# A fused FFT convolution, mixture of experts and bilinear layer: the inverse table is transposed on chip, and steps are placed anew

## The chip, the cores and the metric

The kernel runs on one core of a Trainium2 chip. The metric is the device time of one execution in microseconds, as the median of several runs. TensorE (PE) multiplies matrices, VectorE (DVE), ScalarE (ACT) and GpSimd (POOL) work on elements, and SyncE (SP) does nothing here but start transfers; ACT and POOL start some too. Each engine works through its own instructions in a fixed order and waits on semaphores for the others.

## The reference

```
# filter: x is (8, 3072, 256), filt_r and filt_i are (1537, 256)
X = rfft(x, axis=1);  y = irfft(X * (filt_r + 1j * filt_i), n=3072, axis=1)
x = y.reshape(24576, 256)

# experts: 8 of them, 768 slots each, filled in the order of the tokens
logits = x @ w_gate
e = argmax(logits);  g = softmax(logits)[e]
out = g * (relu(x @ w1[e]) @ w2[e])  if the token got a slot, else 0

# last layer, on all 24576 rows
result = ((out @ w_a) * (out @ w_b)) @ w_out
```

All numbers are f32. A row of zeros stays zero in the last layer.

## The kernel before

With 768 slots for each expert, the first tokens fill all of them. The kernel therefore filters and routes only the first three batches (`NB0 = 3`, 9216 tokens), works on the 6144 tokens that have slots, and writes zeros elsewhere. It counts on the way that every expert is full; if one is not, `general_path` does the rest. In these runs `fast_path` does all.

**The filter.** A transform of 3072 points is one of 128 points (step A, a product with `wa`) and one of 24 points (step B, tables `wb`). A batch has two halves of 128 channels each, and a half has eight chunks of four frequency pairs. For a chunk, `fwd` (L309) makes the spectrum with `wb`, DVE multiplies it with the filter in three instructions (L320 to L322, tiles `fr` and `fi`), POOL adds the two products into `y` (L323), and `inv` (L332) goes back with the tables `wbi`. `idft_t` (L373) turns the result and makes the logits with `iw`, and `idft_a` (L390) is the way back through step A, whose result goes to memory as `rows`. Batch 0 is transformed straight from chip memory (`dft_a_direct`, L277, and transposes with `ident`, L300); batches 1 and 2 go through memory (`dft_a`, L264, tile `da`).

**The loads.** `p1_loads` gives the transfers in the order in which SP starts them. Here they stand one behind another: half of x of batch 0, the tables of its first chunks, the other half, the other tables (four each of `wb` and `wbi`), the filter, small constants, and then batch 1 of x. Each filter tile `fr` has its real part twice, in partitions 0 to 63 and 64 to 127; the second copy is made by ACT (`twice`, L215), but for the first tile of either half, which has one row of its own and is loaded again from `fr0` (L213).

**The order of the work.** It is written out by hand. `seq` is a list of steps i, each with a forward chunk and, two steps later (`LAG`), the way back of the same chunk; three steps after batch 0 have no forward chunk (`GAP`). `put(first, last, ...)` spreads other work evenly over steps first to last: the loads of x, step A of the next batch, and for a finished batch the rest of its filter, its routing and its slots. Routing (`route`, steps s0 to s5) finds the expert and the slot of each token; a scan (s2, L426) counts tokens, s2b (L433) adds counts of other partitions. Slots are entered by eight pairs of `put` (one-hot masks and values on DVE and POOL, L468 to L471) and `add` (a product on PE, L480, and an addition on DVE, L483). When two batches are done, `early_slots` gives the first block of the first three experts, so that they can start while batch 2 is routed.

**The experts.** There are 16 blocks of 384 slots, each of eight steps s. A step makes one chunk of 128 hidden units, in three products for each f32 product (high and low parts, L666 to L668). `load_block` fetches rows with gathers on POOL (L646) and turns them on PE (L657); `load_chunk` loads weights and splits them on ACT (L633) and POOL (L634). Before the first step a list `main` has the last eight steps of `idft_t` of batch 2 with the first gather and turns; the lists `beside[s]` have what is left of batch 2: twelve row products `a`, routing `r`, slots `p` and `d`. From step 17 the weights of the last layer are converted beside the experts, and then comes the last layer.

## Time and profile before

| what | value |
|---|---|
| median of 3 runs | 1127.32 us (1125.75 to 1127.71) |
| profiled execution | 1124.34 us |
| its span, first to last instruction | 1122.5 us |
| busy: PE, PE's weight loads | 95%, 91% |
| busy: DVE, ACT, POOL | 74%, 39%, 60% |
| chain of waits that ended last | PE 80%, DMA 6%, DVE 4%, POOL 2% |

The profile is of one execution, and times in it are counted from the start of its span. It lists, among other things, windows of time with each engine's busy share and PE's granted clock (1.00 is 2.4 GHz, 0.5 is 1.2 GHz), the waits of each engine with what ended them, and the chain of work that ended last, followed back from the end. In the filter and expert stages PE has most work, in the last layer PE is busy nearly without a break.

The filter of the three batches takes up to some 225 us of the span, the experts up to some 540 us, the last layer the rest.

### The profile page before, as it was taken

To read this page: it belongs to the slowest core of one execution; us is meant where nothing else is said; L and a number is where in the kernel's file an instruction comes from. 1 tells how busy PE (TensorE), PEld (TensorE's weight loads), DVE (VectorE), ACT (ScalarE), POOL (GpSimd) and SP (SyncE) were. 2 spreads that over 40 slices of the span, in tenths; PEclk is the share of its full clock that TensorE was granted. 3 is DMA by queue.
4 is the path that set the end of the run, shared out by engine and by line. 5 is a ranking of instruction groups with operands and counts; after the bars stand their busy time and mean duration, and the time that the engine had idled before them with its cause. 6 is when DMAs were issued, how large, how long until landed. Compare 5 with 4: busy or idle time off the path is not lost.

```text
span 1122.5 us, 19362 instructions
## 1 busy us (share of the span) xinstructions
PE 1068.8 (95%) x6908; PEld 1023.9 (91%) x6908; DVE 828.7 (74%) x1589; ACT 442.6 (39%) x894; POOL 673.9 (60%) x676
## 2 busy tenths in 40 slices
PE   7899998899998999999999999999999999999993
PEld 7777797869998999999899999999999999999992
DVE  1738788675575777663888888888888888888873
ACT  2664544454665555553322232232232223232220
POOL 1412645576899787751555756657567475675742
PEclk8999999999999999999999999999999999999997
DMA  9955824354777666550404013040030000100000
GB/s 217 216 198 175 260 60 162 112 188 119 237 229 216 214 199 198 166 178 28 154 1 141 30 43 113 15 142 29 17 140 15 29 29 3 42 15 1 29 1 31
DMA packets 109097, 123.27 MB, mean 110 GB/s; under 512 B 8576, under 2 KB 92544, under 8 KB 108992
## 3 DMA queue, kind: packets, MB, share of 16 engines
q1 hardware_dynamic: 93152, 87.34, 26.4%
q10 hardware_dynamic: 11232, 22.02, 5.4%
q0 software_dynamic: 4608, 12.59, 3.6%
q8 instruction: 56, 0.92, 0.3%
q14 instruction: 49, 0.40, 0.1%
HBM read 68.44 MB, written 53.48 MB: 109 GB/s over the span
## 4 chain that ended last, share of the span: by engine, by line
PE 80%; DMA 6%; DVE 4%; issue 4%; POOL 2%; SPq 1%; ACT 1%; ACTq 0%; DVEq 0%; POOLq 0%
PE ps L666 13%; PE ps L667 13%; PE ps L668 13%; PE po L831 6%; PE po L830 6%; PE po L829 5%; PE yp L667 3%; PE yp L668 3%; PE yp L666 3%; PE ps L373 3%; PE ps L332 3%; PE ps L309 3%; PE ps L390 2%; PE ps L264 2%; DMA fr<-fr 1%
## 5 line engine op out<-in xcount | busy, mean ns | idle before, releaser
L758 POOL TENSOR_TENSOR gl<-w_b,gh 128x384 fp32r<-128x384 f32 x190 | 194.3, 1033 | 196.0 <-ACT gh L757 195.8
L757 ACT CAST gh<-w_b 128x384 fp32r<-128x384 f32 x192 | 98.7, 514 | 262.3 <-DVE w_b L776 196.8
L831 PE MATMUL po<-w_outh,gl 128*128 128x256 f32 x576 | 160.6, 279 | 0.2 <-POOL gl L758 0.2
L830 PE MATMUL po<-w_outl,gh 128*128 128x256 f32 x576 | 160.8, 279 | 0.0
L829 PE MATMUL po<-w_outh,gh 128*128 128x256 f32 x552 | 154.0, 279 | 0.0
L323 POOL TENSOR_TENSOR y<-t,t 112x512 f32<-112x512 f32 x48 | 65.6, 1368 | 128.0 <-DVE t L322 100.7
L634 POOL TENSOR_TENSOR wl<-raw,wh 128x512 fp32r<-128x512 f32 x88 | 112.3, 1292 | 39.6 <-ACT wh L633 16.5
L666 PE MATMUL ps<-th,w_bh 128*128 128x384 f32 x336 | 114.7, 341 | 4.4 <-DVE w_a L769 4.4
L666 PE MATMUL ps<-th,w_ah 128*128 128x384 f32 x336 | 113.5, 338 | 1.3 <-DVE w_b L769 0.8
L667 PE MATMUL ps<-tl,w_ah 128*128 128x384 f32 x336 | 113.6, 338 | 1.0 <-DVE tl L723 0.5
L668 PE MATMUL ps<-th,w_al 128*128 128x384 f32 x336 | 113.3, 337 | 0.0
L667 PE MATMUL ps<-tl,w_bh 128*128 128x384 f32 x336 | 113.2, 337 | 0.0
L668 PE MATMUL ps<-th,w_bl 128*128 128x384 f32 x336 | 113.1, 337 | 0.0
L683 DVE SCALAR_TENSOR_TENSOR hl<-ps,hh 128x384 fp32r<-128x384 f32 x128 | 70.5, 553 | 55.6 <-ACT hh L682 44.6
L831 PEld LDWEIGHTS po<-w_outh,gl 128*128 128x128 f32 x576 | 108.1, 188 | 1.5 <-POOL gl L758 0.4
L830 PEld LDWEIGHTS po<-w_outl,gh 128*128 128x128 f32 x576 | 108.0, 187 | 0.0
L829 PEld LDWEIGHTS po<-w_outh,gh 128*128 128x128 f32 x552 | 103.6, 188 | 0.0
L682 ACT ACTIVATE hh<-ps 128x384 fp32r<-128x384 f32 x128 | 62.7, 490 | 94.3 <-PE ps L668 84.3
L790 ACT COPY p<-ps 128x384 f32<-128x384 f32 x96 | 46.0, 479 | 127.3 <-PE ps L668 69.9
L776 POOL TENSOR_TENSOR w_b<-w_b,w_a 128x384 f32<-128x384 f32 x94 | 93.8, 1019 | 0.0
L666 PE MATMUL ps<-xh,wh 128*128 128x384 f32 x256 | 91.1, 356 | 0.0
L667 PE MATMUL yp<-hl,wh 128*128 128x384 f32 x256 | 86.0, 336 | 3.9 <-DVE hl L683 3.9
(157 smaller groups left out, 2801.3 us busy)
## 6 DMA issues: line engine op xcount, KB each, us to landing
out<-wide SPq DMA_DIRECT2D x48, 512.0 KB
raw<-w SPq DMA_DIRECT2D x176, 128.0 KB
rows<-yt ACTq DMA_DIRECT2D x18, 512.0 KB
da<-sa ACTq DMA_DIRECT2D x12, 512.0 KB
sb<-da SPq DMA_DIRECT2D x32, 192.0 KB
yd<-yb ACTq DMA_DIRECT2D x16, 384.0 KB
y<-yd SPq DMA_DIRECT2D x8, 768.0 KB
sd<-x SPq DMA_DIRECT2D x12, 256.0 KB
```

Source lines behind the costliest of these rows:

```text
L323: eng.tensor_tensor(y, t1, t2, ALU.add)
L634: (eng or nc.gpsimd).tensor_tensor(l, T["raw"], h.bitcast(F32), ALU.subtract)
L666: mm(out, wh, xh, start=first, stop=False)
L667: mm(out, wh, xl, start=False, stop=False)
L668: mm(out, wl, xh, start=False, stop=last)
L683: nc.vector.scalar_tensor_tensor(hl, hp[:, :BLK], 0.0, hh.bitcast(F32), ALU.max, ALU.subtract)
L757: nc.scalar.copy(gh, g)
L758: (v if hurry and not ij[1] else nc.gpsimd).tensor_tensor(gl, g, gh.bitcast(F32), ALU.subtract)
L776: (v if hurry or ij in ON_V else nc.gpsimd).tensor_tensor(c, c, T["a"][ij], ALU.mult)
L829: mm(out, gh[:, sl], oh[:, o:o + D], start=False, stop=False)
L830: mm(out, gh[:, sl], ol[:, o:o + D], start=False, stop=False)
L831: mm(out, gl[:, sl], oh[:, o:o + D], start=False, stop=u == NU - 1 and i == 1 and j == 0)
```

## The change

It has three parts.

*The loads.* The four `wbi` tables are not loaded. The forward table is scaled (by the square root of 2 at one frequency group) so that the way back uses its transpose, and `back_table` makes each `wbi` tile from the `wb` tile with eight transposes on PE and two copies out of PSUM on DVE. It is put into steps 1 to 8, one table in every second step. The second load of the two first filter tiles is replaced by a copy on ACT and the load of a single row, on ACT's queue. Loads of x and of tables stand in another order, and the second half's step A of batch 0 moves from steps 0 to 5 to steps 3 to 6.

*Batch 1.* Its row products and routing go from four steps to six, its slot values and additions from four to six, and `early_slots` moves by three steps to the last one.

*The experts' first steps.* The first block's turns go behind all of `idft_t`, the logits and two row products. In the lists `beside`, the row products go to one per step, the routing moves by three steps, the slot values by four, the additions by five, the gather of the third block from step 2 to step 7, and `all_slots` from step 11 to step 14.

```
-                wb[:, g, 0, 0, 0, q] = c
-                wb[:, g, 0, 1, 0, q] = -sn
-                wbi[0, 0, q, 0, :, g] = 2 * c
-                wbi[1, 0, q, 0, :, g] = -2 * sn
+                wb[:, g, 0, 0, 0, q] = 2 ** 0.5 * c
+                wb[:, g, 0, 1, 0, q] = -2 ** 0.5 * sn
...
         def real(h, i):
             t = self.fr[4 * h + i]
             q.dma_start(t[0:64], io["fr"][:, h, 8 * i:8 * i + 8, :])
+            self.twice[h, i] = lambda: twice(t, h, i)
+
+        def twice(t, h, i):
+            self.nc.scalar.copy(t[64:P], t[0:64])
             if i == 0:
-                q.dma_start(t[64:P], io["fr0"][:, h])
-            else:
-                self.twice[h, i] = lambda: self.nc.scalar.copy(t[64:P], t[0:64])
+                self.nc.scalar.dma_start(t[64:65, 0, :], io["fr0"][:, h])
...
-                steps += [lambda i=i: table("wb", i)] * (h == 0)
+                steps += [lambda i=i: table(i)] * (h == 0)
                 steps += [lambda h=h, i=i: real(h, i)] * (h + i > 0)
                 steps += [lambda h=h, i=i: imag(h, i)]
-                steps += [lambda i=i: table("wbi", i)] * (h == 0)
...
+    def back_table(self, i):
+
+        nc = self.nc
+        for k in range(0, 8, 4):
+            pt = self.ps()
+            for j in range(4):
+                nc.tensor.transpose(pt[0:M2, 96 * j:96 * j + 96], self.wb[i][:, k + j, :], self.ident[0:96, 0:96])
+            nc.vector.tensor_copy(self.wbi[i][:, k:k + 4, :].rearrange("p j r -> p (j r)"), pt[0:M2, 0:384])
...
-            if c % 2 and (h, c // 2 + 1) in self.twice:
-                self.twice.pop((h, c // 2 + 1))()
+            if c % 2 and divmod(4 * h + c // 2 + 1, 4) in self.twice:
+                self.twice.pop(divmod(4 * h + c // 2 + 1, 4))()
...
-        for step in loads[:6]:
+        for step in loads[:3] + consts[:2] + [lambda: K.twice.pop((0, 0))()] + loads[3:6]:
             step()
         K.ident_ids()
-        for step in consts[:5] + loads[6:] + consts[5:]:
+        for step in consts[2:7] + loads[6:9] + consts[7:10] + loads[9:] + consts[10:]:
             step()
...
-        put(0, 5, K.dft_a_direct(xs, sa, 1))
+        put(3, 6, K.dft_a_direct(xs, sa, 1))
+        put(1, 8, [lambda i=i: K.back_table(i) for i in range(4)])
...
-                put(5, 7, xl)
+                put(8, 10, xl)
...
-                put(i + 2, i + 5, rows_and_routes(a, r))
-                put(i + 6, i + 9, p, into=early)
-                put(i + 8, i + 11, d)
-                put(i + 12, i + 12, [K.early_slots, lambda: K.counts(r1, 0, NE, min(cap, BLK))])
+                put(i + 2, i + 7, rows_and_routes(a, r))
+                put(i + 8, i + 13, p, into=early)
+                put(i + 10, i + 15, d)
+                put(i + 15, i + 15, [K.early_slots, lambda: K.counts(r1, 0, NE, min(cap, BLK))])
...
         for k in range(8):
-            main += t1[k:k + 1] + {0: cs[0:1], 1: cs[1:2], 3: first[1:2], 4: first[2:3], 5: cs[2:3],
-                                   6: xs[1][0:1], 7: r[0:1] + cs[3:4]}.get(k, [])
+            main += t1[k:k + 1] + {0: cs[0:1], 2: cs[1:2], 5: cs[2:3], 6: xs[1][0:1]}.get(k, [])
+        main += r[0:1] + a[0:2] + first[1:2] + cs[3:4] + first[2:3]
...
-        beside[2] += xs[2][0:1]
-        for k, step in enumerate(a):
-            beside[k * 2 // 3].append(step)
+        beside[7] += xs[2][0:1]
+        for k, step in enumerate(a[2:]):
+            beside[k].append(step)
         for k, step in enumerate(r[1:]):
-            beside[k].append(step)
+            beside[3 + k].append(step)
         for k in range(0, NPUT, 2):
-            beside[7 + k // 2] += d[k:k + 2]
-            beside[6 + k // 2] += p[k:k + 2]
-        beside[11] += [lambda: K.all_slots(r1), lambda: K.counts(r1, 1, E, cap)]
+            beside[10 + k // 2] += p[k:k + 2]
+        for k in range(NPUT):
+            beside[12 + k // 3] += d[k:k + 1]
+        beside[14] += [lambda: K.all_slots(r1), lambda: K.counts(r1, 1, E, cap)]
```

The first place is the head of SP's queue. `sd` is x of batch 0, `fr`, `fi` and `wb` are the filter and the tables. Before:

```order
L249 DMA sd_89<-x 128x4x128 x6
L165 DMA ident_72<-eye 128x128
L166 DMA ids_69<-ids 128x24
L211 DMA fr0_127<-fr 64x1024
L213 DMA fr0_127<-fr0 64x1024
L207 DMA wb0_119<-wb 96x896
L219 DMA fi0_135<-fi 48x1024
L207 DMA wbi0_123<-wbi 112x768
L249 DMA sd_89<-x 128x4x128 x6
L207 DMA wb1_120<-wb 96x896
L211 DMA fr1_128<-fr 64x1024
```

After:

```order
L247 DMA sd_89<-x 128x4x128 x3
L199 DMA fr0_127<-fr 64x1024
L247 DMA sd_89<-x 128x4x128 x3
L153 DMA ident_72<-eye 128x128
L154 DMA ids_69<-ids 128x24
L195 DMA wb0_119<-wb 96x896
L209 DMA fi0_135<-fi 48x1024
L195 DMA wb1_120<-wb 96x896
L199 DMA fr1_128<-fr 64x1024
L209 DMA fi1_136<-fi 48x1024
L247 DMA sd_89<-x 128x4x128 x3
L195 DMA wb2_121<-wb 96x896
```

The two second copies `fr0` and the tables `wbi` are gone from the queue, the first filter tile stands among x, and the second table stands ahead of the second half of x.

The second place is PE's first chunks of batch 0. `sa0` is the result of step A, `sb` a chunk of it, `y` the filtered spectrum. Before:

```order
L309 MATMUL ps2_242<-sb_228,wb0_119 112x128 x4
L277 MATMUL ps_253<-wa_87,sd_89 128x128 x4
L300 MATMUL ps2_260<-ident_72,sa0_109 96x128 x4
L309 MATMUL ps_267<-sb_235,wb0_119 112x128 x4
L277 MATMUL ps2_278<-wa_87,sd_89 128x128 x4
L300 MATMUL ps_285<-ident_72,sa0_109 96x128 x4
L309 MATMUL ps2_291<-sb_259,wb1_120 112x128 x4
L332 MATMUL ps_303<-wbi0_123,y_248 128x96 x4
L277 MATMUL ps2_309<-wa_87,sd_89 128x128 x4
L300 MATMUL ps_316<-ident_72,sa0_109 96x128 x4
L309 MATMUL ps2_323<-sb_284,wb1_120 112x128 x4
```

After:

```order
L307 MATMUL ps2_238<-sb_224,wb0_119 112x128 x4
L298 MATMUL ps_250<-ident_72,sa0_109 96x128 x4
L307 MATMUL ps2_257<-sb_231,wb0_119 112x128 x4
L232 MATMUL ps_268<-ident_72,wb0_119 112x96 x4
L232 MATMUL ps2_274<-ident_72,wb0_119 112x96 x4
L298 MATMUL ps_281<-ident_72,sa0_109 96x128 x4
L307 MATMUL ps2_287<-sb_249,wb1_120 112x128 x4
L330 MATMUL ps_299<-wbi0_123,y_244 128x96 x4
L298 MATMUL ps2_306<-ident_72,sa0_109 96x128 x4
L307 MATMUL ps_313<-sb_280,wb1_120 112x128 x4
L275 MATMUL ps2_324<-wa_87,sd_89 128x128 x4
L330 MATMUL ps_330<-wbi0_123,y_263 128x96 x4
```

The products of step A (`wa`) have left these steps, and the first table's transposes (L232, from `wb0`) stand between the second forward chunk and the third; the first product of the way back, `wbi0`, stands behind the third forward chunk as before, and its table is now made and not loaded.

The third place is PE's handover from the filter to the experts. `sc` is the filtered result of batch 2, `rowt` the gathered rows, `xh` and `xl` their parts. Before:

```order
L373 MATMUL ps_2081<-iw_111,sc_1787 128x136 x3
L373 MATMUL ps2_2087<-iw_111,sc_1787 128x136 x3
L657 MATMUL ps_2093<-ident_72,rowt_2028 128x128 x3
L373 MATMUL ps2_2099<-iw_111,sc_1787 128x136 x3
L657 MATMUL ps_2105<-ident_72,rowt_2028 128x128 x3
L373 MATMUL ps2_2111<-iw_111,sc_1787 128x136 x3
L373 MATMUL ps_2121<-iw_111,sc_1787 128x136 x3
L373 MATMUL ps2_2139<-iw_111,sc_1787 128x136 x3
L412 MATMUL ps_2145<-z_1755,wai_110 128x192 x2
L390 MATMUL ps_2165<-sd_1756,wai_110 128x512
L390 MATMUL ps_2168<-sd_1756,wai_110 128x512
L666 MATMUL ps_2179<-xh_2038,wh_2067 128x384
```

After:

```order
L371 MATMUL ps_2139<-iw_111,sc_1804 128x136 x3
L371 MATMUL ps2_2145<-iw_111,sc_1804 128x136 x3
L371 MATMUL ps_2155<-iw_111,sc_1804 128x136 x3
L371 MATMUL ps2_2173<-iw_111,sc_1804 128x136 x3
L410 MATMUL ps_2179<-z_1777,wai_110 128x192 x2
L388 MATMUL ps2_2186<-sd_1778,wai_110 128x512
L388 MATMUL ps_2189<-sd_1778,wai_110 128x512
L655 MATMUL ps2_2193<-ident_72,rowt_2074 128x128 x3
L655 MATMUL ps_2203<-ident_72,rowt_2074 128x128 x3
L388 MATMUL ps_2218<-sd_1778,wai_110 128x512
L664 MATMUL ps_2221<-xh_2084,wh_2113 128x384
L665 MATMUL ps_2221<-xl_2085,wh_2113 128x384
```

The two turns with `ident` stood among the `iw` products; now they stand behind the last of these, behind the logits and two row products with `wai`.

## Rows read from the trace of the kernel before

**Rows 1.** Windows: busy time of each engine, granted clock, DMA share, GB/s.

```profile
core 0: us, PE busy (x) PEld busy (x) DVE busy (x) ACT busy (x) POOL busy (x), PEclk, DMA share, GB/s
24.00:52.00 28.00, 24.62 (x220) 24.23 (x220) 20.62 (x30) 19.34 (x29) 12.66 (x10) 1.00 0.96 195
162.00:212.00 50.00, 45.67 (x317) 39.03 (x315) 45.41 (x90) 20.48 (x38) 24.52 (x28) 0.97 0.31 100
188.00:196.00 8.00, 6.75 (x46) 6.75 (x46) 6.38 (x11) 1.51 (x4) 7.00 (x10) 0.79 0.07 19
214.00:285.00 71.00, 65.08 (x369) 56.51 (x368) 40.37 (x90) 36.31 (x78) 51.78 (x52) 1.00 0.53 165
```

**Rows 2.** DMA issues by line: tiles, queue, number of transfers, size of each.

```profile
fr<-fr SPq DMA_DIRECT2D x10, 256.0 KB
wbi<-wbi SPq DMA_DIRECT2D x4, 336.0 KB
```

**Rows 3.** Chain of waits at batch 1's first products: start us, us, what.

```profile
50.79 4.22 DMA sd<-x
55.15 3.75 PE ps L264 x4
...
60.30 1.75 PE ps L264 x4
```

**Rows 4.** Timeline of PE, one chunk: start us, us, instructions, idle before.

```profile
42.55 0.60 PE L300 MATMUL ps<-ident,sa 128*96 128x128 f32 x4
42.99 1.04 PE L309 MATMUL ps<-sb,wb 96*112 96x128 f32 x8
43.86 1.03 PE L332 MATMUL ps<-wbi,y 112*128 112x96 f32 x8
```

**Rows 5.** Timeline of DVE: first filter product, two consecutive chunks, a PSUM copy.

```profile
17.29 0.69 DVE L320 SCALAR_TENSOR_TENSOR t<-ps,fi 48x512 f32<-48x512 f32 x1 [16.13 <-PE ps L309]
...
41.95 0.69 DVE L320 SCALAR_TENSOR_TENSOR t<-ps,fi 48x512 f32<-48x512 f32 x1
...
44.12 0.69 DVE L320 SCALAR_TENSOR_TENSOR t<-ps,fi 48x512 f32<-48x512 f32 x1
...
81.12 0.55 DVE L378 COPY sd<-ps 128x384 f32<-128x384 f32 x1
```

**Rows 6.** Timeline of PE and ACT: first way-back product, first second copy.

```profile
26.11 1.03 PE L332 MATMUL ps<-wbi,y 112*128 112x96 f32 x8
...
27.08 1.04 ACT L215 COPY fr<-fr 64x1024 f32<-64x1024 f32 x1 [5.68 <-DMA fr<-fr]
```

**Rows 7.** Waits of PE, 0 to 270 us: us in total, times, longest us.

```profile
PE ps L264 <- DMA sd<-x: 4.6, 1, 4.6
...
PE ps L332 <- POOL y L323: 3.4, 1, 3.4
PE ps L433 <- DVE tot L428: 2.7, 1, 2.7
PE ps L657 <- DMA rowt<-rows,early: 1.9, 2, 1.3
```

**Rows 8.** The three scans (ns min/median/max), and POOL's timeline at the third.

```profile
L426 DVE TENSOR_TENSOR_SCAN cum<-scm,oh x3: 548/559/4741, 98.9 to 229.8; 128x192 f32<-128x192 f32 x3
...
229.13 4.95 POOL L634 TENSOR_TENSOR wl<-raw,wh 128x512 fp32r<-128x512 f32 x4
```

**Rows 9.** Handover: last sum y, third gather in the chain, first expert product.

```profile
212.69 1.28 POOL L323 TENSOR_TENSOR y<-t,t 112x512 f32<-112x512 f32 x1 [1.16 <-DVE t L322]
...
216.94 4.40 DMA rowt<-rows,early
...
226.91 0.74 PE L666 MATMUL ps<-xh,wh 128*128 128x384 f32 x1
```

**Rows 10.** Timeline of POOL and ACT: gather of the fourth block, cast of its rows.

```profile
279.22 1.03 POOL L646 DMA_INDIRECT rowt<-rows,gidx  x1 [0.15 <-issue]
...
288.48 0.48 ACT L658 CAST xh<-ps 128x384 fp32r<-128x384 f32 x1 [0.37 <-PE ps L657]
```

26 lines of the change are left out of this document (8 added, 18 removed).

## The prediction

> **What bounds the kernel now.** The page's busy shares came first: PE is busy 95% of the span, and the chain of waits that ended last is 80% PE. So an edit pays only where PE stands still or runs at its lower clock, and the question is where it does. The windows show three places before the experts are in full swing, and the change touches all three. The list of PE's waits names what ended them [rows 7].
>
> First place, the end of the loads: PE waits 4.6 us for batch 1 of x [rows 7], whose first tile lands at 50.79 + 4.22 = 55.0 us; the four products after that take 3.75 us, and the same four a little later 1.75 us [rows 3]: 2.0 us more, at the lower clock. All queues were full until then, with a DMA share of 0.96 at 195 GB/s [rows 1], so fewer bytes mean an earlier batch 1.
>
> Second, 162 to 212 us: PE is idle for 4.3 of 50 us, and from 188 to 196 its mean clock is 0.79, worth another 8 x 0.21 = 1.7 us. But VectorE (DVE) is busy 45.41 us there [rows 1]. PE's largest wait is 3.4 us, for POOL's sum, which stands behind DVE's products [rows 7]: DVE is the bound here, with 4.6 us left to gain at most.
>
> Third, the handover to the experts: 1.9 us for gathered rows and 2.7 us for the total of a scan [rows 7]. What PE waits for later than that the change leaves alone.
>
> **Part 1, the loads.** Four wbi tables of 336 KB and two copies of 256 KB go [rows 2]: 1.90 MB, at 195 GB/s [rows 1] 9.7 us of queue. Batch 1's first tile would land near 45.5 us. What is late next is PE itself, since it gets work. I follow PE from the first product of the way back, which starts at 26.11 us [rows 6], to batch 1's first product, for which PE is ready at 55.15 - 4.6 = 50.6 us [rows 3, 7]: 24.5 us.
>
> That first product now waits for its table, and the table for DVE. DVE's first filter product starts at 17.29 us [rows 5]; the first wb table comes earlier, but a ScalarE copy of 1.04 us [rows 6] now stands ahead of the first chunk, and I let these cancel (bounds: 1.5 us either way). Then DVE must do two chunks of 2.17 us (the period of L320) and two PSUM copies of 0.55 us [rows 5]: 17.3 + 4.3 + 1.1, with 0.5 for hops, 23.2 us. That is 2.9 us sooner than now, because chunk 2 no longer waits for its late forward table.
>
> Behind it PE gets more: six of the eight groups of four transposes, priced as the existing group that starts at 42.55, with the next instruction at 42.99 [rows 4]: 6 x 0.44 = 2.6 us. And two groups of step A, which used to lie ahead of that point, at the 0.87 us of a group of four [rows 4]: 1.7 us. So PE is ready at 23.2 + 24.5 + 4.4 = 52.1 us, by then the tile has long landed, and PE has not idled, so that the slow products go too. In place of 55.15 + 2.0 = 57.2 us: **5.1 us gained**. Bounds: 9.7 if the transposes and copies find idle time everywhere, 0 if DVE's eight extra copies (8 x 0.55 = 4.4) go in full onto its chain. The extra copy for the second half and the one-row load on ScalarE's queue have cover: PE is ahead of ScalarE by a chunk there. A load on SP that reuses that row's semaphore can wait for ScalarE; 6 us of margin between 45.5 and 52.1 hide it.
>
> **Part 2, batch 1's rows and slots.** No work goes or comes; twelve row products and the routing are spread from four chunks over six, the slot products from four over six. DVE's load per chunk falls where it piled up, and PE is no longer blocked while DVE catches up. Since DVE binds, the gain is DVE's own idle time, 0 to 4.6 us [rows 1]; I take two thirds, **3 us**, because a piece of the idle time is chunks in which the row products kept PE from feeding DVE, and that is what the spreading ends.
>
> The slot table now closes with the last chunk, so the first gather starts later against the last forward chunk. In the kernel before, the last sum y ends at 212.69 + 1.28 = 213.97 us and the third gather lands at 216.94 + 4.40 = 221.34 [rows 9]: 7.4 us. The expert's first product starts at 226.91, 12.9 us after y, and 1.9 of it is the wait for the gather. The change puts all of the idft steps, the logits and two row products ahead of the turns. Without the wait and the 2 us or so of turns and splits, 9 us of PE work cover 7.4 us of gather. So **1.9 us gained**; the cover is 1.6 us, and beyond it the gather is late and the gain goes (bounds 0 and 1.9).
>
> **Part 3, the experts' first steps.** The scan takes 4.74 us instead of 0.56 because, as the rows stand, it runs through four POOL splits in a row, 4.95 us [rows 8]; PE waits 2.7 us for what follows it [rows 7]. POOL had those four splits queued up behind gathers. After the change the scan comes at step 4, one step ahead of its use as now, and the gather for the third block is at step 7, so POOL should have two splits at a time and not four: 2 x 1.24 = 2.5 us of blocking in place of 4.95. I take **1.7 us** of the 2.7 as gained (bounds 0 and 2.7).
>
> The Trainium skill (SBUF — State Buffer, Who interferes with whom) says that DVE and GpSimd share one port pair under an exclusive lock held for one whole instruction. By that the scan would lose at most one split, about 1.2 us, and no wait would be left: 2.7 instead of 1.7. The row speaks against it, as the scan sat out four.
>
> Against that, slot products move from steps 6 to 9 to steps 10 to 13, nearer to the step-14 gather. That gather starts at 279.22 and its rows are cast at 288.48 [rows 10], 9.3 us for a gather that needs about 7.4 (above): nearly 2 us of lead. POOL is busy 51.78 of 71 us in this part [rows 1], and PE's time there shrinks by some 4. I put **0.8 us lost** (bounds 0 and 3).
>
> **The sum.** 5.1 + 3 + 1.9 + 1.7 - 0.8 = 10.9 us. The profiled execution took 1124.34 us, span 1122.5 and 1.84 around it; it would become 1113.4. The median of the runs, 1127.32, lies 2.98 above that execution, so the median would be 1116.4.
>
> **Rivals.** *DVE stays the bound.* It has 45.4 us of work for 50 us, and its work is the same; if spreading only moves the waits, part 2's 3 us are lost, and with them part 3's gain, as POOL has the same work in less time: 5.1 + 1.9 - 0.8 = 6.2, so 1121.1 us. For it speaks that DVE's work per chunk with slot products is as long as PE's.
>
> *The loads were hidden, or PE's new work takes the gain.* If the first table waits for DVE and each later one too, part 1 gives nothing: 10.9 - 5.1 = 5.8, so 1121.5 us. Against it: PE stood idle for 4.6 us there and the table copies are one chunk ahead of their use from chunk 4 on.
>
> *More than forecast.* PE idles nowhere up to the loads' end (8 us gained), DVE closes its gaps (4.6), the scan does not wait (2.7): 8 + 4.6 + 1.9 + 2.7 = 17.2, so 1110.1 us.
>
> *Slower: the clock stays low.* Before batch 1, PE now waits for a chain through DVE and does transposes among its products. If the granted clock stays at 1.2 GHz instead of 2.4 from the first chunk to the end of that stage, the 34 us of PE work from 17 to 52 us take twice as long. The gain of 5.1 turns into a loss of about 29, and with the other 5.8 gained the time is some 1150 us. A clock that is low for only part of it costs half of that stretch; it decides above 22 us at the low clock (half of which is the whole 10.9). Against it: with a transpose group in each step, 24 to 52 us runs at clock 1.00 and PE is busy 24.62 of 28 us [rows 1].
>
> The Trainium skill (TensorE: Matmul & The Clock Gate, Part 4: PE-mode transpose) says that transposes do not count as activity of PE for the clock as products do, which would favour this rival. The same row is evidence that a mix with products keeps the clock.
>
> **How the numbers follow.** Forecast (1112.5 to 1119.5): 0.58. DVE stays the bound: 0.16. Load gain lost: 0.10. More: 0.08. Slower by the clock: 0.05. The rest, 0.03, is a gain eaten by things not seen here. The range goes from 1109, the rival with more, to 1122.5, past the two with about half the gain; the slow clock is left out. A measurement of this kernel tells about 0.2%, 2.3 us, from no change. Faster: 0.58 + 0.16 + 0.10 + 0.08, less a little for rivals added to each other, 0.90; slower 0.06; same 0.04.
>
> **What would show it.** Right: no wait of PE on x before its first product on batch 1, which starts near 52 us at full clock; the first way-back product near 23 us; a window of 50 us before the last chunk with DVE idle for under 2.5 us; no wait on the early gather; the wait on the scan's total under 1.2 us. Wrong: that wait on x still there; a granted clock near 0.5 after 24 us; a PE wait of over 2 us on the gather of the fourth block.

## The result, and the profile after

| | before | after |
|---|---|---|
| median (executions) | 1126.53 us (4; 1124.44 to 1127.71) | 1110.46 us (4; 1109.49 to 1111.44) |
| profiled execution, its span | 1124.34 us, 1122.5 us | 1111.44 us, 1109.7 us |
| ratio after : before, 95% interval | | 0.9859, 0.9840 to 0.9879 |

The change gains 15.9 us (13.6 to 18.0). Forecast were 10.9 us and a median of 1116.4; 1110.46 lies in the range of 1109 to 1122.5, near its lower end, but below the 1112.5 to 1119.5 that had most of the chance. The sign and the places were right, the sizes too small.

PE's waits up to 270 us in the changed kernel (in total, times, longest); left out are 1.2 us at the start, which the kernel before has too, and two waits of 0.2 us. Lines are numbered two lower than before.

```profile
PE ps L330 <- POOL y L321: 2.2, 3, 1.1
PE ps L330 <- DVE wbi L233: 1.7, 1, 1.7
PE ps L298 <- ACT sa L276: 1.4, 2, 0.7
PE ps L275 <- DMA sd<-x: 1.3, 2, 1.0
...
PE ps L478 <- POOL val L468: 1.1, 1, 1.1
...
```

Against [rows 7], batch 1 of x, the scan's total and the early gather are gone from the list, and so are 2.9 us for forward tables (PE's L309 on `wb`, which [rows 7] leaves out); POOL's sum `y` costs 2.2 us in three waits instead of 3.4 in one. What came in their place is 1.7 us for the first table made on chip, and 1.1 us for slot values from POOL.

The first way-back product and batch 1's first product on PE, and DVE's first filter product and its first copies of a table:

```profile
21.37 1.86 PE L330 MATMUL ps<-wbi,y 112*128 112x96 f32 x8 [1.69 <-DVE wbi L233]
...
51.33 1.88 PE L262 MATMUL ps<-sd,wa 128*128 128x512 f32 x4
```

```profile
16.50 0.69 DVE L318 SCALAR_TENSOR_TENSOR t<-ps,fi 48x512 f32<-48x512 f32 x1 [15.35 <-PE ps L307]
...
20.67 1.01 DVE L233 COPY wbi<-ps 112x384 f32<-112x384 f32 x2
```

Windows of the changed kernel. The last one is the 50 us before its last forward chunk.

```profile
core 0: us, PE busy (x) PEld busy (x) DVE busy (x) ACT busy (x) POOL busy (x), PEclk, DMA share, GB/s
20.00:24.00 4.00, 2.63 (x13) 2.63 (x14) 3.72 (x7) 1.21 (x2) 1.37 (x3) 0.69 1.12 237
24.00:28.00 4.00, 4.00 (x34) 4.00 (x33) 2.07 (x3) 1.20 (x3) 1.35 (x2) 0.88 1.17 219
24.00:52.00 28.00, 27.32 (x243) 26.66 (x242) 19.93 (x31) 18.90 (x29) 10.39 (x9) 0.98 0.93 207
148.53:198.53 50.00, 48.21 (x359) 42.03 (x358) 45.82 (x91) 22.96 (x45) 26.23 (x28) 1.00 0.35 109
```

And the three scans (ns min/median/max), with POOL's splits beside the third:

```profile
L424 DVE TENSOR_TENSOR_SCAN cum<-scm,oh x3: 548/548/627, 92.7 to 226.0; 128x192 f32<-128x192 f32 x3
```

```profile
224.95 2.78 POOL L632 TENSOR_TENSOR wl<-raw,wh 128x512 fp32r<-128x512 f32 x2 [1.74 <-ACT wh L631]
```

The way back starts at 21.37 us instead of 26.11 [rows 6], batch 1 at 51.33 and at once at full speed, four products in 1.88 us instead of 3.75 [rows 3]. The third scan takes 0.63 us instead of 4.74, beside two splits instead of four [rows 8].

**Where the time came from.** Four marks can be followed through all kernels: DVE's first filter product of chunk 36 (of 48, counted from 0) and of the last chunk, 47; the 15th residual `hl` of the experts; and the last of the 128 `hl`. Before, then after, the range at the end of the last row being the first and the last start:

```profile
163.27 0.69 DVE L320 SCALAR_TENSOR_TENSOR t<-ps,fi 48x512 f32<-48x512 f32 x1 [0.30 <-PE ps L309]
...
210.43 0.69 DVE L320 SCALAR_TENSOR_TENSOR t<-ps,fi 48x512 f32<-48x512 f32 x1
...
277.24 0.56 DVE L683 SCALAR_TENSOR_TENSOR hl<-ps,hh 128x384 fp32r<-128x384 f32 x1 [1.52 <-ACT hh L682]
...
L683 DVE SCALAR_TENSOR_TENSOR hl<-ps,hh x128: 535/554/558, 229.3 to 529.2; 128x384 fp32r<-128x384 f32 x128
```

```profile
157.05 0.69 DVE L318 SCALAR_TENSOR_TENSOR t<-ps,fi 48x512 f32<-48x512 f32 x1 [0.30 <-PE ps L307]
...
198.53 0.69 DVE L318 SCALAR_TENSOR_TENSOR t<-ps,fi 48x512 f32<-48x512 f32 x1
...
261.82 0.56 DVE L681 SCALAR_TENSOR_TENSOR hl<-ps,hh 128x384 fp32r<-128x384 f32 x1 [0.15 <-ACT hh L680]
...
L681 DVE SCALAR_TENSOR_TENSOR hl<-ps,hh x128: 541/557/560, 217.4 to 516.2; 128x384 fp32r<-128x384 f32 x128
```

The lead is 6.2 us at the first mark and has been so, to 0.05 us, since chunk 12, the first one after step A of batch 1 has begun (the expectations below call it batch 1's second chunk; it is one of batch 0's second half). Up to there it goes up and down: 6.4 us at chunk 2, as the way back starts earlier, and -0.9 at chunks 8 to 11, when PE has done the work that the change adds. It comes back between chunks 11 and 12, where the kernel before waits 4.6 us for x and loses 2.0 at the lower clock. It grows by 5.7 to the last chunk, by 3.5 to the 15th residual, and shrinks by 2.4 to the end of the experts: 13.0 us, as the profiled executions differ (12.9). The same marks in all kernels that were run, from one profile of each, in us against that one profile of the kernel before (the last column to 0.1 us):

| kernel | ratio to before (95%) | lead at chunk 36 | gained to chunk 47 | gained to 15th residual | lost to last residual |
|---|---|---|---|---|---|
| the change | 0.9859 (0.9840 to 0.9879) | 6.2 | 5.7 | 3.5 | 2.4 |
| loads_only | 0.9957 (0.9935 to 0.9978) | 8.8 | -1.0 | -4.7 | 0.7 |
| spread_only | 0.9974 (0.9955 to 0.9993) | 1.1 | 5.7 | -2.8 | 1.9 |
| steps_only | 0.9945 (0.9927 to 0.9963) | -1.8 | -1.2 | 4.1 | 1.7 |
| no_loads | 0.9892 (0.9862 to 0.9923) | 0.9 | 5.7 | 3.5 | 2.8 |
| one_table | 0.9853 (0.9829 to 0.9876) | 4.2 | 5.7 | 3.5 | 3.7 |
| bytes_back | 0.9868 (0.9839 to 0.9897) | 7.7 | 5.7 | 3.6 | 0.2 |
| tables_loaded | 0.9901 (0.9871 to 0.9930) | 0.2 | 5.7 | 3.5 | 2.6 |
| gather_at_2 | 0.9871 (0.9844 to 0.9898) | 7.0 | 5.7 | -1.4 | 1.7 |
| slots_early | 0.9904 (0.9875 to 0.9934) | 6.3 | 5.7 | -3.1 | 2.7 |
| slots_four | 0.9881 (0.9859 to 0.9903) | 6.8 | 2.6 | 4.1 | 1.5 |
| x_first | 0.9832 (0.9805 to 0.9858) | 3.9 | 5.7 | 3.5 | 1.3 |
| act_x | 0.9830 (0.9802 to 0.9858) | 8.0 | 5.7 | 3.6 | 2.3 |

With the spreading, the gain to chunk 47 repeats to 0.1 us in ten kernels, and with the new steps too that to the 15th residual in seven; without them they scatter. So does the lead at chunk 36. Four kernels have the loads of before: 0, 1.1, -1.8 and 0.9, mean 0.1. Five have the changed ones as they are: 6.2, 8.8, 7.0, 6.3 and 6.8, mean 7.0. In the last column every kernel loses against that profile of before, the kernels with the old loads too, and nearly all of it between the 51st and the 61st residual. Both kernels wait 1.8 us for `hl` there; in the kernel before the granted clock stays at 1.00, in the changed kernel it falls:

```profile
348.00:352.00 4.00, 4.00 (x15) 3.90 (x15) 2.42 (x6) 1.32 (x3) 4.00 (x3) 0.50 0.42 128
```

The profiled execution of before, at 1124.34 us, is quicker than its four others, and the changed kernel's is the slowest of its four. So 7.0 + 5.7 + 3.5 = 16.2 us is a better account of the medians' 15.9 than the pair of profiles.

### The profile page after: what moved, and what is told of

Read it like the earlier page. It is cut to its first block, busy times and chain, and to the rows that moved or that the text cites. A ratio compares the mean times of both kernels' runs of the same rounds, so it can differ in the third digit from the quotient of the medians.

```text
span 1109.7 us, 19438 instructions
## 1 busy us (share of the span) xinstructions
PE 1067.3 (96%) x6940; PEld 1024.6 (92%) x6940; DVE 831.1 (75%) x1597; ACT 444.9 (40%) x896; POOL 675.6 (61%) x676
```

## The experiments

**One part at a time.** The three parts of the change were put on the kernel before, each alone. loads_only has Part 1. Of the diffs the core is shown, and `...` marks what is left out:

```
-                steps += [lambda i=i: table("wbi", i)] * (h == 0)
...
+        put(1, 8, [lambda i=i: K.back_table(i) for i in range(4)])
```

> The kernel before with Part 1 of the change alone: the table of the way back made on chip, one row instead of the 256 KB copies, the new order of the loads, step A of the first batch later. Measured from chunk to chunk, the filter products of VectorE in the changed kernel run 6.2 us ahead of the kernel before from batch 1's second chunk up to chunk 36. Theory (the three parts add up): with this part alone the lead is the same 6.2 us at those chunks and is kept to the end, so the time falls by 6.2 us. Rival (VectorE as the bound of the stage before the last chunk swallows a lead): VectorE has 45 us of work for 50 us there, so part of the lead is lost between chunk 37 and the last, and 2 to 4 us are left at the end. Second rival (the lead is given back at the handover, where gathers and splits were the bound): PE's waits on gathered rows and on the scan grow by the lead, 0 to 2 us left.

spread_only has the spreading of batch 1:

```
-                put(i + 2, i + 5, rows_and_routes(a, r))
-                put(i + 6, i + 9, p, into=early)
...
+                put(i + 2, i + 7, rows_and_routes(a, r))
+                put(i + 8, i + 13, p, into=early)
...
```

> The kernel before with the spreading of batch 1's row products, routing and slot products alone. In the changed kernel this stretch, from chunk 37 to the last, gains 5.7 us over the kernel before. Theory (it needs the new order of the experts' first steps): the slot table closes three chunks later, with the last chunk, and the first gather follows it; in the kernel before's order the turns and the first splits come before the row products, so PE has little left to do while the gather runs. The 5.7 us are gained up to the last chunk, and PE then waits for the gathered rows some 5 to 7 us in place of 1.9: the time falls by 0 to 3 us. Rival (the parts add up): the wait stays near 1.9 us and the time falls by 5 to 6 us. Rival (VectorE stays the bound, as named in the prediction): no lead at the last chunk, and the time gets longer by the later gather.

steps_only has the experts' first steps:

```
+        main += r[0:1] + a[0:2] + first[1:2] + cs[3:4] + first[2:3]
...
-        beside[2] += xs[2][0:1]
...
+        beside[7] += xs[2][0:1]
...
```

> The kernel before with the new order of the experts' first steps alone, row products ahead of the turns, the third block's gather and the scan later, slot products later. Theory (it mends waits only): PE's wait of 1.9 us on the gathered rows and of 2.7 us on the scan's total go, and what is late next takes a little of it: the time falls by 2 to 4 us. Rival (it brings nothing by itself, since in the changed kernel the experts' part gained 0.8 us and the handover 0.3): the time falls by 0 to 1.2 us, and the waits are only replaced by other idle time of PE between the last chunk and the fourth block.

Measured: 4.8 us (2.5 to 7.3), 2.9 us (0.8 to 5.1) and 6.2 us (4.2 to 8.2) faster. The sum, 13.9, can't be told from the whole change's 15.9.

The loads alone lead by 8.8 us at chunk 36 and have 2.4 left at the end of the experts. The interval of the medians leaves room for the theory (6.2 us) and for the first rival. The second rival is right that this execution loses at the handover, but not how: PE doesn't wait longer there than before. From the last chunk to the 15th residual, before, after, and with the loads alone:

```profile
210.43:277.24 66.81, 60.75 (x352) 51.91 (x352) 39.93 (x89) 34.62 (x75) 47.72 (x48) 1.00 0.54 170
198.53:261.82 63.29, 61.14 (x363) 52.81 (x363) 41.30 (x96) 34.27 (x75) 49.13 (x50) 1.00 0.57 177
202.63:274.15 71.52, 65.40 (x356) 56.52 (x356) 41.09 (x89) 34.76 (x75) 47.41 (x48) 0.93 0.51 159
```

PE is idle for 6.1 us before and for 6.1 with the loads alone. The 4.7 us that are lost are PE's own work, 65.40 us in place of 60.75, at a clock of 0.93 in place of 1.00. In the changed kernel the clock stays at 1.00 and PE is idle for 2.2 us. The longer of the two waits with the loads alone, on DVE, POOL and PE:

```profile
221.40 6.07 DVE L419 TENSOR_TENSOR oh<-eio,am 128x192 f32<-128x192 f32 x1
```

```profile
222.01 4.97 POOL L632 TENSOR_TENSOR wl<-raw,wh 128x512 fp32r<-128x512 f32 x4
```

```profile
227.91 2.07 PE L388 MATMUL ps<-sd,wai 128*128 128x512 f32 x2 [2.59 <-DVE hl L681]
```

POOL's four splits take 4.97 us, and DVE's mask `oh` lasts 6.07 us across them (0.63 in the profile of before). Behind it stands `hl`, for which PE waits 2.59 us, and after that the granted clock was 0.50 from 228 to 232 us. In the kernel before the same row of splits fell on the scan, the next step of the routing; PE waited 2.7 us for its total, and the clock stayed at 1.00.

The spreading alone has its 5.7 us at the last chunk and gives half back, as its theory said, but the wait for the gather is 3.1 us, not 5 to 7 (the line below). In all PE is idle for less time there than before, 4.8 us; behind the wait the clock was 0.50 from 216 to 220 us, and 0.95 up to the 15th residual.

```profile
PE ps L657 <- DMA rowt<-rows,early: 3.1, 3, 1.2
```

The new steps alone end both waits, of 1.9 and 2.7 us, and gain more than was expected, 6.2 us; their profiled execution, 1125.05 us, is the slowest of the twelve and shows less. The rival, 0 to 1.2 us, is out.

**Parts 2 and 3 together.** no_loads is the changed kernel with the loads of the kernel before; of its diff:

```
-        put(3, 6, K.dft_a_direct(xs, sa, 1))
-        put(1, 8, [lambda i=i: K.back_table(i) for i in range(4)])
+        put(0, 5, K.dft_a_direct(xs, sa, 1))
```

> The changed kernel without Part 1 (loads and tables as before), that is, the spreading of batch 1 and the new order of the experts' first steps together. Alone these two gave 2.9 and 6.2 us, and Part 1 alone 4.8; the whole change about 16. Theory (in the loads' stage and at the handover the time hangs on the clock that PE is granted after it stood idle, and the new order leaves no idle stretch at the handover to give the lead back): Part 1 is worth 6 to 8 us in the company of the others, so this kernel is 8 to 10 us faster than the kernel before. Rival (the parts add up): Part 1 is worth 4.8 us here too, and this kernel is 11 us faster. Rival (Part 1 and the spreading do the same work twice, since both feed VectorE earlier): this kernel is 13 us or more faster.

Measured: 12.2 us (8.7 to 15.6), which leaves all three cases open. The marks say more: 5.7 and 3.5 us, as in the changed kernel, so neither stretch hangs on the loads. The spreading costs 2.8 us at the handover by itself and the new steps give 4.1 by themselves, but with them the spreading's later table costs only 0.6.

**What of the loads it is.** Three edits of the changed kernel. one_table makes one of the tables and uses it for all four:

```
-        put(1, 8, [lambda i=i: K.back_table(i) for i in range(4)])
+        put(1, 8, [lambda: K.back_table(0)])
```

> The changed kernel with one of the four tables of the way back made on chip and used in place of all four; six of the eight groups of transposes and six of the copies out of PSUM are left out. This prices the work that the change adds. Theory (PE binds up to batch 1's first product): six groups at 0.33 us of PE, 2.0 us, fall out of the time, and the first way-back product still comes at 21.4 us. Rival (the transposes and copies lie in idle time): no change within 0.5 us. Rival (VectorE binds there): six copies at 0.55 us, 3.3 us, fall out.

bytes_back adds transfers of the size of the dropped tables:

```
+            if h == 0:
+                extra = self.drm.tile([96, 8, M2], F32, name=f"extra{i}")
+                q.dma_start(extra, io["wb"][:, 8 * i:8 * i + 8, :])
```

> The changed kernel with 1.34 MB of extra transfers, four of 344 KB from the table of the way there into a spare place in device memory, put on SyncE's queue where the four dropped tables stood. Nothing waits for them; the tables are still made on chip. Theory (it is the bytes): at some 200 GB/s the loads end 6 to 7 us later, PE waits again for batch 1 of x by 1 to 5 us, and the time rises by 4 to 7 us, with the slow products that follow the wait. Rival (it is the order: the first way-back product no longer stands behind the second forward table, and x comes with a margin of more than 6 us): the time rises by at most 1.5 us, and there is no wait on batch 1 of x.

tables_loaded loads the tables of the way back again:

```
+            if h == 0:
+                q.dma_start(self.wbi[i], io["wbi"][:, 8 * i:8 * i + 8, :])
...
-        put(1, 8, [lambda i=i: K.back_table(i) for i in range(4)])
```

> The changed kernel with the four tables of the way back loaded, 336 KB each, as in the kernel before, and not made on chip; the one row in place of the 256 KB copies, the order of the loads, step A and all else stay as changed. In four profiles with Part 1 as changed, the filter products from batch 1's second chunk to chunk 36 run 6.2 to 8.8 us ahead of the kernel before, 7.1 on average; extra transfers within device memory took none of that. Theory (the tables made on chip are what the loads' gain comes from): with them loaded the lead there falls to 2 us or less, PE waits on batch 1 of x again for 3 us or more, and the time rises by 5 us or more. Rival (the row, the order of the loads and step A's place are the gain; the tables on chip only move the work): the lead stays at 6 us or more and the time within 1.5 us. A lead between, 3 to 5 us, divides it.

One table instead of four gains 16.6 us (14.0 to 19.3), which can't be told from 15.9. What the added work costs is read from PE's busy time between the first way-back product and batch 1's first, for which PE was ready at 50.57 us before; then come loads_only, which does all eight groups, and one_table, in whose execution everything is later, as batch 0's x came late (a wait of 2.4 us):

```profile
26.11:50.57 24.46, 23.68 (x214) 23.26 (x212) 18.59 (x27) 18.30 (x28) 10.18 (x8) 1.00 0.98 203
20.46:48.77 28.31, 27.62 (x253) 27.26 (x253) 21.71 (x34) 18.96 (x28) 10.99 (x9) 1.00 0.94 208
24.00:53.22 29.22, 27.21 (x228) 26.79 (x228) 18.90 (x28) 18.65 (x28) 10.95 (x9) 0.94 0.83 179
```

At the same clock, six groups of transposes and two of step A take 3.9 us more (28.31 - 24.46), and PE has hardly more idle time to hide them in, 0.8 us before and 0.7 after. Six groups at 0.33 us are 2.0 of it. In one_table PE's work, without some 1.7 us for four microseconds at 0.59, is 25.5 us, 2.1 less than in loads_only: the theory that PE binds has the size of the work. But that execution gives 1.3 us of it back: PE is idle for 2.0 us, all for ScalarE's copies of step A, and ScalarE had waited for a late filter tile, whose second copy stands ahead of them in its queue:

```profile
38.47 1.04 ACT L203 COPY fr<-fr 64x1024 f32<-64x1024 f32 x1 [3.51 <-DMA fr<-fr]
```

In the eight other profiles with the tables made on chip that wait is 0.68 us.

Extra transfers within device memory cost little: the lead is 7.7 us, and 14.9 us (11.6 to 18.2) are gained. Up to chunk 11 this execution runs as loads_only's to 0.01 us. Then PE waits 0.87 us before batch 1's first product:

```profile
49.80 1.96 PE L265 MATMUL ps<-sd,wa 128*128 128x512 f32 x4 [0.87 <-DVE t L321]
```

The profile names DVE's product at 49.04 us, but loads_only, whose DVE has the same product at 49.04, starts on batch 1 at 48.77, before it. So the wait is for x, issued at 45.66 us in place of 43.41, and the lead is 1.1 us smaller. The rival holds in size, not in that there is no wait.

The same tables loaded into chip memory cost the whole lead (0.2 us left, in one execution) and 4.7 us of the medians, with intervals that just overlap (7.9 to 14.6 us gained). So the row in place of the 256 KB copies and the new order give nothing without the tables made on chip that this profile shows. The theory of tables_loaded holds for the lead, misses the time by a little (5 us or more), and names the wrong place. PE does not wait for batch 1 of x; it waits for the second half of batch 0, for what ScalarE makes of it, and for forward tables (1.9 us), and loses clock behind that:

```profile
PE ps L312 <- ACT sa L290: 3.7, 2, 3.0
PE ps L289 <- DMA sd<-x: 3.3, 3, 2.5
...
```

```profile
16.00:32.00 16.00, 12.07 (x90) 11.50 (x90) 8.32 (x13) 4.08 (x6) 5.06 (x4) 0.89 1.11 223
```

ScalarE's part is again a second copy that waits for its filter tile, 7.85 us here and 4.95 at the next one, with step A's copies behind it:

```profile
31.28 1.04 ACT L215 COPY fr<-fr 64x1024 f32<-64x1024 f32 x1 [7.85 <-DMA fr<-fr]
```

The 16 us from 16 to 32 with the extra transfers in device memory:

```profile
16.00:32.00 16.00, 14.32 (x134) 14.14 (x133) 13.12 (x21) 8.60 (x13) 6.35 (x5) 1.00 1.09 272
```

At the same DMA share the loads into chip memory move 223 GB/s, and with the others beside them 272. So the loads' gain comes from tables that are not loaded, but, as far as one profile of each tells, it is not one of bytes alone. Why transfers within device memory found room there, the runs don't show.

**Who is late next: x, or PE.** SP in the changed kernel at x of batch 1; the nine small constants ahead of it start at 39.17 us:

```profile
45.81 3.65 SPq L247 DMA_DIRECT2D sd<-x  x6
```

x_first puts x ahead of them (its diff moves `load_x` besides), and act_x, whose further edit follows, has the first table's copies on ScalarE as well:

```
-        for step in consts[2:7] + loads[6:9] + consts[7:10] + loads[9:] + consts[10:]:
+        for step in consts[2:7] + loads[6:9] + consts[7:10] + loads[9:] + consts[10:-9] + xl + consts[-9:]:
```

> The changed kernel with batch 1 of x on SyncE's queue ahead of the nine small constants instead of behind them. In the changed kernel the first of x is issued at 45.81 us, after nine small loads from 39.17 us on, and PE takes up batch 1 at 51.33 us; in two of four profiles of the same code PE waited 0.5 to 0.6 us for x. Theory (PE itself is late next, as the prediction had it): x is issued near 39 us, lands by 45, no wait on x remains, and the time falls by 0.6 us at most; the lead over the kernel before at chunk 12 to 36 stays within 6.2 to 8.8 us. Rival (the margin was used up and x still sets the end of this stage): the lead grows to over 9.5 us and the time falls by 2 us or more.

```
-            nc.vector.tensor_copy(self.wbi[i][:, k:k + 4, :].rearrange("p j r -> p (j r)"), pt[0:M2, 0:384])
+            copy = nc.scalar.copy if i == 0 else nc.vector.tensor_copy
+            copy(self.wbi[i][:, k:k + 4, :].rearrange("p j r -> p (j r)"), pt[0:M2, 0:384])
```

> The changed kernel with x ahead of the constants, and with the first table of the way back copied out of PSUM by ScalarE instead of VectorE. In all profiles with the tables made on chip PE waits 1.7 us for the first table at 19.7 to 21.4 us, since VectorE's copies stand behind the second chunk's products; in one of them the granted clock then fell to 0.69 and 0.88 for the next 8 us. Theory (the VectorE copies of the first table set the start of the way back): the wait falls under 0.5 us, the first way-back product comes 1.2 us or more earlier, the clock stays at 1.00 from 16 to 52 us, and the lead at chunk 12 to 36 is 8.5 to 10 us; the time falls by 1 to 3 us against the changed kernel. Rival (PE's work up to batch 1 is bound by ScalarE's copies of step A's second half): PE's waits on those copies, 1.4 us now, grow by what the table gives, and the time stays within 1 us.

With x issued first, at 41.52 us, no wait on it is left; the lead at chunk 36 is 3.9 us, outside both forecasts, since batch 0's x came late in that execution (waits of 2.2 us) and the clock was 0.58 from 24 to 28 us. With the copies on ScalarE too, PE's wait for the table and the window after it are

```profile
20.30 1.10 PE L331 MATMUL ps<-wbi,y 112*128 112x96 f32 x8 [0.69 <-ACT wbi L234]
```

```profile
20.00:24.00 4.00, 3.71 (x34) 3.73 (x34) 3.85 (x6) 2.28 (x5) 2.35 (x2) 1.00 1.09 225
```

0.69 us instead of 1.69, the way back starts 1.1 us earlier, the clock stays at 1.00 up to 52 us, and the lead is 8.0 us: each a little short of what was expected (under 0.5, 1.2 or more, 8.5 or more), and no more than loads_only has without it. PE's waits on ScalarE's copies of step A stay at 1.4 us, so the rival is out. 19.0 and 19.2 us faster than before are the best medians of all, but their intervals (16 to 22 us) overlap the changed kernel's, so that they are better is not shown. What they show is that x doesn't set this stage any more, by more than the 0.5 to 0.9 us that three other executions waited for it.

**The scan and POOL's splits.** gather_at_2 undoes one line of the change:

```
-        beside[7] += xs[2][0:1]
+        beside[2] += xs[2][0:1]
```

> The changed kernel with the third block's gather back at the experts' step 2 instead of 7; all else as changed. In the changed kernel the scan takes 0.63 us and PE doesn't wait for its total; POOL has one or two splits in a row there. Theory (POOL's splits pile up behind the gathers, and a VectorE operation between SBUF tiles sits out the whole row of them): POOL runs three or four splits in a row around the scan's chain, one VectorE operation there takes 4 to 6 us instead of about 1, PE waits 2 to 3 us more, and the time rises by 2 to 3 us. Rival (one split at most is sat out, wherever the gather stands): the scan's chain gets longer by under 1.3 us and the time by under 1 us.

The scan on DVE, POOL's splits beside it, PE's wait, and PE's clock behind that:

```profile
225.22 5.70 DVE L424 TENSOR_TENSOR_SCAN cum<-scm,oh 128x192 f32<-128x192 f32 x1
```

```profile
224.29 6.20 POOL L632 TENSOR_TENSOR wl<-raw,wh 128x512 fp32r<-128x512 f32 x5
```

```profile
231.27 0.36 PE L431 MATMUL ps<-tot,tri 128*128 128x8 f32 x2 [2.94 <-DVE tot L426]
```

```profile
232.00:236.00 4.00, 4.00 (x14) 3.76 (x15) 1.67 (x6) 1.00 (x2) 0.70 (x1) 0.61 0.16 52
```

Five splits in a row take 6.20 us, and the scan that starts 0.9 us into them ends 0.4 us after them: 5.70 us. PE waits 2.94 us and then runs four microseconds at 0.61. Up to the 15th residual this loses 3.5 + 1.4 = 4.9 us against the changed kernel; the medians say 1.3 us, with intervals that overlap, so the 2 to 3 us of the theory are not shown in the time. In the row, the scan and the wait the theory holds, the rival with one split does not.

**The slots.** slots_early puts the last batch's routing and slots back to the steps of before:

```
-            beside[3 + k].append(step)
+            beside[k].append(step)
...
-            beside[10 + k // 2] += p[k:k + 2]
...
+            beside[6 + k // 2] += p[k:k + 2]
...
```

> The changed kernel with the last batch's routing and slot products back at the experts' steps of the kernel before (routing from step 0 instead of 3, slot products from 6 instead of 10, the slot table at 11 instead of 14); the gather at step 7 and the row products ahead of the turns stay. Theory of the prediction (slot products near the gather of the fourth block delay it): 0.8 us are gained back, up to 3, and PE's wait on that block's gather, 2.2 us in the changed kernel, shrinks below 1.5. Rival (the scan's chain meets POOL's run of three splits at step 1): PE waits 1 to 3 us for the scan's total, and the time rises by 1 to 3 us. Rival (neither matters, as PE is 15.4 us ahead of the kernel before from the first steps to the fourth block, and gives back 2.4 us only behind it, to gathers and splits on POOL): within 0.7 us.

It loses 3.5 + 3.1 = 6.6 us up to the 15th residual, and 5.1 in the medians. PE's waits there, POOL at the longer one, and PE's clock behind both:

```profile
PE ps L478 <- POOL val L468: 2.5, 1, 2.5
PE ps L431 <- DVE tot L426: 1.8, 1, 1.8
```

```profile
243.82 1.00 POOL L644 DMA_INDIRECT rowt<-rows,early  x1 [0.30 <-issue]
```

```profile
224.00:228.00 4.00, 4.00 (x16) 3.24 (x16) 2.63 (x5) 1.29 (x3) 1.40 (x1) 0.75 0.00 0
248.00:252.00 4.00, 4.00 (x17) 3.52 (x17) 2.42 (x6) 1.00 (x2) 2.86 (x5) 0.76 0.24 66
```

Three gathers of the third block, at step 7, of which the last is shown, now stand ahead of slot values that PE wants; the first of these starts on POOL at 244.85 us. With 1.8 us for the scan's total, 4.3 us of waits, and a clock of 0.75 and 0.76 behind each. The time moves against the prediction's theory; the rival with the scan's chain names the smaller half of the loss. The 2.2 us that the expectation gives as the changed kernel's wait on the fourth block's gather are waits on later blocks, at 326 and 347 us, where the kernel before waits 1.8 us too; on the fourth block's gather PE waits neither in those two kernels nor in this one. As the gather at step 7 is part of the loss, this run does not price early slots beside a gather at step 2.

slots_four does so for batch 1's slots, and leaves its row products spread:

```
-                put(i + 8, i + 13, p, into=early)
-                put(i + 10, i + 15, d)
-                put(i + 15, i + 15, [K.early_slots, lambda: K.counts(r1, 0, NE, min(cap, BLK))])
+                put(i + 8, i + 11, p, into=early)
+                put(i + 10, i + 13, d)
+                put(i + 14, i + 14, [K.early_slots, lambda: K.counts(r1, 0, NE, min(cap, BLK))])
```

> The changed kernel with the last piece of the spreading undone: batch 1's slot products over four chunks again instead of six, and the slot table closed one chunk earlier; the row products and the routing stay spread over six. From chunk 36 to the last chunk the spreading gains 5.7 us in each of seven profiles that have it. VectorE's busy time in that stretch is 43.2 us of 47.2 before and 39.8 of 41.5 after: 3.4 us less work, since slot products moved behind the last chunk, and 2.2 us less idle time. Theory (VectorE is the bound, and it is the work moved behind the last chunk that pays): the gain in the stretch falls to 2.5 to 4 us, as the slot products are back before the last chunk, and the gathers stand up to 2 us nearer to it; at the experts the time is 1 to 3 us longer than the changed kernel's. Rival (it is the row products that no longer block PE): the stretch still gains 5 us or more, and the time stays within 1 us. Rival (neither, the later table costs as much at the handover as the stretch gains): the stretch gains 2.5 to 4 us and the lead at the experts is the changed kernel's within 0.5 us.

From chunk 36 to the last one, before, after, and with four chunks of slots:

```profile
163.27:210.43 47.16, 42.98 (x295) 36.53 (x294) 43.22 (x86) 19.04 (x34) 23.12 (x27) 0.96 0.30 101
```

```profile
157.05:198.53 41.48, 39.69 (x284) 33.51 (x283) 39.77 (x77) 19.27 (x35) 22.77 (x25) 1.00 0.39 121
```

```profile
156.44:201.04 44.60, 41.24 (x292) 34.59 (x291) 41.33 (x80) 19.02 (x35) 23.73 (x27) 1.00 0.35 110
```

The gain falls to 2.6 us, and 2.5 us of time go (13.4 us faster than before, 10.9 to 15.9, which overlaps the changed kernel's interval). DVE's busy time is 43.22, 39.77 and 41.33 us. So more than half of the stretch's gain hangs on the slot products, and the theory's numbers hold.

Its reason holds in part. Of the 3.4 us of DVE's time that the change takes out of the stretch, some 2.5 us are work moved behind the last chunk: four of the eight additions (1.0), the step on `ids` that ends them (1.0) and three small ones. The rest is work that stays and takes less time in sum, such as the masks of the slot values. Before, then after:

```profile
L468 DVE TENSOR_TENSOR val<-line,hi 128x144 f32<-128x144 f32 x8 | 4.5, 561 | 1.5 <-PE ps L480 1.5
L466 DVE TENSOR_TENSOR val<-line,hi 128x144 f32<-128x144 f32 x8 | 3.7, 466 | 0.0
```

In slots_four these masks take 560 ns again, and of its 3.1 us only 0.5, two additions, are work that comes back into the stretch; 1.1 are longer masks, and 1.6 idle time of DVE.

## Why the prediction was right, and where it was too small

**The bound** was read rightly: three places where PE stands still, and all three gave time.

**Part 1**, 5.1 us forecast, about 7.0 measured. Its mechanism held: PE is what is late, batch 1's first product comes at 51.33 us (52.1 forecast) without a wait for x and at full speed. The terms were off in size. The way back starts 1.8 us earlier than the 23.2 forecast: DVE's first product came 0.8 us sooner, and the product on PE needs only the first of two copies. The work added behind that, 4.4 us in the forecast, took 3.9 in loads_only, which has no stretch at a low clock there: a group of transposes is 0.33 us and not 0.44. In the changed kernel's own execution 1.7 us at a low clock come on top. And the step that had the tile "long landed" from 45.5 us on was wrong: x is issued only at 45.81 us, and with the same loads gather_at_2 and slots_early waited 0.6 and 0.5 us for it; the 6 us of margin were none. Of the 9.7 us of queue, 5.0 became an earlier x, which was issued at 50.79 before [rows 3].

**Part 2** is the step that failed: "the gain is DVE's own idle time, 0 to 4.6 us". The stretch gave 5.7 us. DVE was the bound, but its busy time did not stay the same ("No work goes or comes"): the spread reaches past the last chunk, where DVE stood idle for 5.2 us in a piece, and DVE's busy time in the stretch falls by 43.22 - 39.77 = 3.4 us, 2.5 of them moved work and the rest work that takes less time; its idle time falls by 2.2 us, from 3.94 to 1.71. The sign named for it, DVE idle for under 2.5 us in the last 50, was therefore not met (50 - 45.82 = 4.2). The 1.7 us at a low clock, which the prediction saw there, went too: the stretch runs at 1.00.

**The handover and Part 3**, 1.9 + 1.7 - 0.8 = 2.8 us forecast, 3.5 measured. The early gather is covered, as worked out, and spread_only shows what it costs without the cover (a wait of 3.1 us). The scan came out at the upper bound: no wait is left. The -0.8 for the later slot products came out near its size in another place: there is no wait for the fourth block's gather, but PE waits 1.1 us for slot values from POOL. 1.9 + 2.7 - 1.1 = 3.5. Of the 5.3 us by which 16.2 exceeds the forecast, Part 1 has 1.9, Part 2 has 2.7 and the rest 0.7.

On the scan the rule of the Trainium skill (SBUF — State Buffer, Who interferes with whom) was weighed against the row: by it the lock is held for one instruction, from which the prediction took that the scan would lose one split at most. gather_at_2 decides: five splits were sat out. In the changed kernel, with splits one or two at a time, two small DVE instructions behind the scan lose nearly one split each (a copy of 128x8 takes 1.08 us, 0.17 in loads_only), which is that size, and the scan itself, which starts 0.2 us before the first of two splits ends, gets in between the two: it takes 0.63 us, and the second split 1.55 in place of 1.28. Where the section says that a DVE instruction with at most one input in SBUF (chip memory), outside the modes that use two ports, does not contend, the trace agrees: `hl`, with its other input from PSUM, takes 0.56 us at 217.41, in the middle of three splits.

**The rivals.** DVE as the bound was true, and did not hinder. PE's added work took 3.9 us, and the rival in which it takes the whole gain did not come. The rival with more than forecast, 17.2 us, was nearest, and it had 0.08; 1110.46 lies in the range because the range was drawn down to that rival. It was near in the sum more than in its reasons, since PE's added work was not hidden. The slow clock showed in part: 0.69 and 0.88 from 20 to 28 us, behind the wait for the table, about 4 x 0.31 + 4 x 0.12 = 1.7 us, and 1.00 from then on. The Trainium skill's rule on transposes (TensorE: Matmul & The Clock Gate, Part 4: PE-mode transpose), which favoured it, made no difference that this case shows: 24 to 52 us has them among the products and runs at 0.98, and in loads_only 20.46 to 48.77 us runs at 1.00.

## What to carry to other kernels

Where an engine binds a stretch, count its work by what has to be done before the stretch's end and not in all: work moved behind the end is gained if the engine idles there, though none of it goes away (2.5 of the 5.7 us here). A step that gathers on POOL drags a queue of other POOL work behind it, so place it where neither DVE's small chains nor POOL's own short results are wanted soon. A copy that waits for a load holds up everything behind it on its engine, as ScalarE's second copies did when their tiles were late. Where two profiles differ in a stretch, look at idle time and clock apart: loads_only idled as long as the kernel before and lost 4.7 us by the clock. And compare marks of the same work in several profiles: one pair of executions was off by 3 us, while the gain of a single stretch repeated to 0.1 us.

## What the runs showed of the hardware

Three DVE instructions with both inputs in chip memory that met a row of POOL's splits waited for all of it: a scan of 0.55 us took 4.74 beside four and 5.70 beside five, a mask of 0.63 took 6.07 beside four. It is not always so: the scan of the changed kernel got in between two splits (0.63 us). Residuals that read PSUM kept their 0.56 us.

After waits of PE of 2.94, 2.59 and 2.5 us the granted clock was 0.61, 0.50 and 0.76 for four microseconds, but after the 2.7 us in the kernel before it stayed at 1.00. The same 1.69 us of waiting for the first table was followed by 0.69 in the changed kernel and 0.58 in x_first, and by 1.00 in loads_only, gather_at_2 and slots_early. So the wait alone does not tell which it will be; where the clock fell, it cost time on top of them (4.7 us of longer work in loads_only, beside 6.1 us of idle time).

Four loads of 336 KB into chip memory cost 7 us of lead, four of the same size within device memory on the same queue some 1 us, in one profile of each.
